# Two attention layers on one core: rounded parts copied ahead of low parts, ScalarE issuing some of the copies, and a longer interleaved tail

## The chip, the cores and the metric

The kernel runs on one core of one Trainium2 chip. The metric is the device time of one execution in microseconds (us); the kernel before has a median of 1974.42 us over three runs (1971.13 to 1975.38). Lower is better.

## The reference, cut to what matters

Two independent attention layers, A and B, each with x of 2048 x 1024, 32 heads of width 32, their own `wqkv` and `wo`. The results stand side by side in the output.

```python
# both: qkv = x @ wqkv, 32 heads of 32; out = attention(q, k, v) @ wo
# A: each query sees 8 keys, 2 apart: pos, pos-2, ..., pos-14  (softmax over those)
# B: each query sees the last 256 keys                         (softmax over those)
return jnp.concatenate([a, b], axis=-1)
```

## The kernel before, in words

**Units.** The work is cut into eight units of 512 positions: four of layer B ("dense", a query sees up to 384 key columns) and four of layer A ("window", 136 key columns; even and odd positions are separated on the host, so 8 keys 2 apart become 8 neighbours). A unit has eight head groups of four heads, so there are 64 head groups, numbered 0 to 63 here in the order of the work. All units but the first of a sequence need the last keys of the unit before, which are kept in a DRAM tile called `halo`.

**Precision by parts.** Every fp32 operand is split into a rounded part and a low part (the remainder). A product is three matmuls (`TERMS`): rounded x rounded, rounded x low, low x rounded. The splitting of inputs is in `Stream.parts` (line 129 the rounding cast on VectorE, lines 134 and 137 the subtraction on GpSimd or VectorE).

**A head group's stages.**

1. Projection (line 363, 24 matmuls of 512 columns for Q and 24 for K). ScalarE writes the rounded part into the tile `nat` (line 314), VectorE the low part (line 318).
2. Stacking (lines 323 to 335). Three DMAs of 256 KB copy `nat` into every third partition of `qst`, three into `kst`. For Q the order is rounded, rounded, low; for K it is rounded, low, rounded. All are issued by SyncE (SP), once both parts of `nat` are counted as done. For K of a unit with a halo, three halo reads (line 308) are issued ahead of them; if the next unit needs it, one halo write (line 333) behind them. If the buffer is still used by the head group two before, the whole stacking is put off (`waiting`).
3. First pass (line 614): sixteen score matmuls (96 rows, up to 384 columns). VectorE finds the row maximum (619), ScalarE the sum of exponentials (624). There are four PSUM banks for scores.
4. Row values: logarithm (637), its parts (642 to 645), a transposing matmul (653), a copy on VectorE (657), and a 16 KB DMA into rows 96 and 97 of `qst` (660, SP).
5. Second pass: scores again, now with the row values (696 dense, 509 window), exponential on ScalarE, masks, and the product with V (741, 548) into PSUM; `finish` writes the parts of the result, `ot` (577, 581).
6. Between these, V projections (line 415) and output projections (line 455; one result copied out through the single buffer `ost`, lines 379 and 382, and stored by a DMA that ScalarE issues, line 470).

**What sets the order.** The order of each engine's instructions is fixed when the program is built. `Clock` is a small cost model: `copy` stands for a DMA that SP issues, `load` for one that ScalarE issues, `fetch` for one of GpSimd. The loop at the end of the kernel takes four lists (row values, second passes, first passes, projections) and puts next on TensorE the item whose modelled ready time comes first. A first pass becomes ready at `done["stack"]`, the modelled landing of K's last copy:

```python
one.append(Item(lambda: latest(rs.when(), done["stack"].get((u, s))),
                lambda b=b, j=j: first(b, j), 0.18 if dense else C1))
```

On the chip TensorE goes through this fixed list. If a copy lands later than modelled, TensorE stands still at that first score matmul although projections are left to do.

**The tail.** The last unit's eight output projections are 24 matmuls each, three per head group. `TAIL` of them have their first seven head groups placed early; the eighth, which needs the last head group's result, follows. The output weights come through `wpool`, three buffers.

Of the kernel before, what the change touches and what calls it, by code (L numbers as in the profile page):

```python
# [14 lines left out]
P = 128  # L15
# [10 lines left out]
O_SLOTS = {2: (0, 1), 3: (2, 3), 4: (4, 5), 5: (6, 7)}  # L26
NX, NST = 10, 1
TAIL, LAND, XAT = 2, 0.45, 1
# [4 lines left out]
class Clock:  # L33
# [53 lines left out]
class Stream:  # L87
# [19 lines left out]
    def split_to(self, n):  # L107
        while self.split < min(n, len(self.items)):
            i = self.split
            self.load_to(i + 1)  # L110
            raw, t0 = self.raw.pop(i)
            if self.items[i][0] == "x":
# [10 lines left out]
            end = self.ready[i] if self.items[i][0] != "x" else max(self.ready[i])  # L123
            self.ck.defer(end, lambda n=i + NRAW + 1: self.load_to(n))
# [22 lines left out]
def kernel(ctx, tc, xs, wqk, wv, wo, outs, units):  # L147
# [23 lines left out]
    for u in range(U):  # L171
        for s in range(NG):
# [3 lines left out]
            if s in V_SLOTS:  # L176
                plan.append(("v", u, V_SLOTS[s]))
# [17 lines left out]
    for p in plan:  # L195
        ly = units[p[1]][0]
        if p[0] == "o":
            item(p, "w", wo[ly, p[2]])
# [99 lines left out]
    def qk_items(u, s):  # L298
# [12 lines left out]
        def evac(t, ps, bank):  # L311
# [5 lines left out]
            def low():  # L317
# [5 lines left out]
                def stack():  # L323
                    if t == 1 and has_halo:
                        read_halo()
                    dst, c = (qst[buf], 0) if t == 0 else (kst[buf], 256)
                    for i, a in enumerate((0, 0, 1) if t == 0 else (0, 1, 0)):
                        nc.sync.dma_start(dst[i:96:3, :, c:c + S].bitcast(F32), hl[:, a, :].bitcast(F32))
# [6 lines left out]
                    done["nat"][hg, t] = e2  # L335

                if hg < 2 or hg - 2 in done["o"]:
                    stack()
                else:
                    waiting.setdefault(hg - 2, []).append(stack)  # L340

            ck.defer(r, low)
# [95 lines left out]
    def o_items(u, n):  # L438
        h = {}

        def ready(k):
            if (u * NG + k) not in done["ot"]:
                return None
            if k == 0:
                st.split_to(where["o", u, n] + 1)
                h["r"] = st.ready[where["o", u, n]]
                return latest(rg.when(), h["r"], done["ot"][u * NG])
            return done["ot"][u * NG + k]

        def run(k):  # L450
            if k == 0:
                h["ps"], h["b"] = rg.take()
                h["w"], _ = st.get(where["o", u, n])
            for i, (a, b) in enumerate(TERMS):
                nc.tensor.matmul(h["ps"], h["w"][:, a, k * P:(k + 1) * P], ot[u, k][:, b, :],  # L455
                                 start=(k == 0 and i == 0), stop=(k == NK - 1 and i == 2))
            if k == 3 and (u < U - 1 or n != TAIL - 1):
                st.split_to(where["o", u, n] + 2)

        def after(k):  # L460
            if k == NK - 1:
# [4 lines left out]
                e = copy_out(o, h["ps"], h["b"], rg)  # L466
# [122 lines left out]
    def attention(u, s):  # L589
# [9 lines left out]
        def first(b, j):  # L599
# [18 lines left out]
            def top():  # L618
                nc.vector.tensor_tensor_reduce(ps[:, :n], ps[:, :n], mask[:, cut:full], scale=-1.0, scalar=BIG,  # L619
                                               op0=ALU.add, op1=ALU.min, accum_out=nm)  # L620
                e = ck.use("dve", (n + 80) / 960, ck.now)
# [29 lines left out]
        def rows(hl):  # L651
# [4 lines left out]
            def copy():  # L656
# [3 lines left out]
                nc.sync.dma_start(q[96:98, :, :].bitcast(F32), rt.bitcast(F32))  # L660
                h["rows"] = ck.copy(0.3, e)
# [212 lines left out]
```

## Time and profile before

| | us |
|---|---|
| median of three runs | 1974.42 |
| the profiled execution | 1973.82 |
| its span, first to last instruction | 1972.1 |
| TensorE busy in it | 1924.7 (12608 matmuls) |
| VectorE, ScalarE, GpSimd busy | 1295.7, 957.5, 708.7 |
| mean granted TensorE clock | 0.987 |

The span is what the profile covers; 1.7 us lie around it. A matmul's time in the profile contains its pipeline, so a busy TensorE is not a full one: what one matmul really takes is the distance from its start to the next one's start. "Idle before" at an instruction is the time for which its engine did nothing, and "<-" names what ended it.

### The profile page before, as it was taken

Reading aid. Unit: us, or ns where it says so; the run is one execution under the profiler, and the core shown is the slowest. Engines: PE = TensorE matmul, PEld = TensorE weight load, DVE = VectorE, ACT = ScalarE, POOL = GpSimd, SP = SyncE. Lnnn points to the kernel's source line nnn. Section 1 sums busy time; section 2 is a strip of 40 time slices with the busy share of each in tenths; the row PEclk is TensorE's granted clock in tenths of the full one; section 3 lists DMA queues with packets and bytes.
Section 4 is the critical chain, followed back from the end, with each engine's and each line's share of the span. In section 5 each row is a group of like instructions: output and inputs, shape, how many; then the busy total and the mean of one; then the engine's idle time right before and its main releaser. Section 6 shows DMA issues by size and latency. Waiting matters only on the chain.

```text
span 1972.1 us, 36479 instructions
## 1 busy us (share of the span) xinstructions
PE 1924.7 (98%) x12608; PEld 1619.8 (82%) x12608; DVE 1295.7 (66%) x3762; ACT 957.5 (49%) x3137; POOL 708.7 (36%) x923
## 2 busy tenths in 40 slices
PE   7999999999999999999999999999999999999998
PEld 6878887888877878788878888978888788888886
DVE  5687776678665786567865657655666557666653
ACT  3565554475654656555563344423534334434441
POOL 4334343444433434443443323233332333233221
PEclk9999999999999999999999999999989999999998
DMA  5555546455546465345645647455553565556442
GB/s 176 150 139 153 160 124 178 132 153 157 152 136 174 121 189 149 117 140 148 177 119 146 173 139 196 128 149 170 149 163 116 174 177 162 141 146 172 136 126 75
DMA packets 136502, 294.92 MB, mean 150 GB/s; under 512 B 14464, under 2 KB 42112, under 8 KB 136320
## 3 DMA queue, kind: packets, MB, share of 16 engines
q1 hardware_dynamic: 85632, 124.82, 26.1%
q0 software_dynamic: 40320, 146.82, 22.9%
q10 hardware_dynamic: 10368, 20.98, 2.9%
q8 instruction: 100, 1.64, 0.4%
q14 instruction: 82, 0.67, 0.1%
HBM read 163.58 MB, written 27.26 MB: 97 GB/s over the span
## 4 chain that ended last, share of the span: by engine, by line
PE 84%; DVE 7%; DMA 6%; ACT 2%; issue 1%; SPq 0%; POOL 0%; DVEq 0%; ACTq 0%; POOLq 0%
PE g L363 31%; PE g L455 16%; PE g L415 16%; PE s L614 7%; PE s L696 5%; PE o L741 4%; PE s L509 3%; DMA qst<-rt 3%; PE o L548 2%; DMA kst<-nat 1%; DMA raw<-xs 1%; DVE x L137 1%; DVE w L129 1%; ACT s L624 1%; DVE w L137 1%
## 5 line engine op out<-in xcount | busy, mean ns | idle before, releaser
L363 PE MATMUL g<-x,w 128*128 128x512 f32 x3072 | 801.9, 401 | 8.6 <-DVE w L129 8.0
L134 POOL TENSOR_TENSOR w<-raw,w 128x512 fp32r<-128x512 f32 x225 | 392.5, 1745 | 897.2 <-PE s L614 285.7
L363 PEld LDWEIGHTS g<-x,w 128*128 128x128 f32 x3072 | 562.0, 191 | 110.9 <-DVE w L129 8.4
L624 ACT ACTIVATE s<-s,nm 128x384 f32<-128x384 f32 (+3 forms) x1024 | 452.3, 443 | 231.0 <-DVE nm L619 227.1
L415 PE MATMUL g<-w,x 128*128 128x256 f32 x3072 | 413.3, 285 | 0.0
L415 PEld LDWEIGHTS g<-w,x 128*128 128x128 f32 x3072 | 392.7, 191 | 1.9 <-issue 0.6
L455 PE MATMUL g<-ot,w 128*128 128x512 f32 x1536 | 384.2, 397 | 3.6 <-DVE w L129 2.9
L455 PEld LDWEIGHTS g<-ot,w 128*128 128x128 f32 x1536 | 283.8, 190 | 58.1 <-DVE w L129 3.6
L619 DVE CUSTOM_DVE_ANT_0 s<-s,mask_d 128x384 f32<-128x384 f32 (+2 forms) x512 | 262.0, 556 | 72.9 <-PE s L614 71.5
L614 PE MATMUL s<-kst,qst 96*128 96x384 f32 (+3 forms) x1024 | 238.7, 303 | 16.2 <-ACT s L624 7.1
L701 ACT ACTIVATE pbuf<-s 128x384 f32<-128x384 f32 (+2 forms) x480 | 197.1, 507 | 85.5 <-PE s L696 81.8
L614 PEld LDWEIGHTS s<-kst,qst 96*128 96x128 f32 x1024 | 181.3, 192 | 60.5 <-ACT s L624 18.1
L624 ACT ACTIVATION_READ_ACCUMULATOR s<-s,nm 128x1 f32 x1024 | 210.2, 205 | 0.0
L619 DVE CUSTOM_DVE_ANT_0 s<-s,mask_w 128x136 f32<-128x136 f32 (+1 forms) x512 | 142.4, 322 | 98.4 <-PE s L614 96.8
L129 DVE CAST w<-raw 128x1024 fp32r<-128x1024 f32 x256 | 199.9, 781 | 9.4 <-PE g L455 9.4
L137 DVE TENSOR_TENSOR w<-raw,w 128x512 fp32r<-128x512 f32 x287 | 197.2, 696 | 8.8
L682 POOL TENSOR_SCALAR_AFFINE_SELECT pbuf<-pbuf 128x128 f32<-128x128 f32 (+1 forms) x383 | 147.9, 404 | 150.1 <-ACT pbuf L701 143.5
L314 ACT ACTIVATE nat<-g 128x512 fp32r<-128x512 f32 x128 | 76.6, 598 | 255.2 <-PE g L363 247.8
L318 DVE SCALAR_TENSOR_TENSOR nat<-g,nat 128x512 fp32r<-128x512 f32 x128 | 88.3, 690 | 145.5 <-ACT nat L314 134.9
L524 DVE TENSOR_TENSOR pbuf<-pbuf,keep_w 128x272 f32<-128x272 f32 (+1 forms) x224 | 116.9, 566 | 61.5 <-ACT pbuf L514 60.6
L619 DVE DVE_READ_ACCUMULATOR2_ANT nm<- 128x1 f32 x1024 | 144.3, 141 | 0.0
L696 PEld LDWEIGHTS s<-qst,kst 98*128 98x128 f32 x704 | 106.2, 189 | 37.8 <-PE o L741 10.0
(48 smaller groups left out, 1227.3 us busy)
## 6 DMA issues: line engine op xcount, KB each, us to landing
raw<-wqk POOLq DMA_DIRECT2D x126, 512.0 KB, 3.7
qst<-nat SPq DMA_DIRECT2D x192, 256.0 KB
kst<-nat SPq DMA_DIRECT2D x192, 256.0 KB
raw<-wo POOLq DMA_DIRECT2D x64, 512.0 KB, 3.7
raw<-wv POOLq DMA_DIRECT2D x62, 512.0 KB, 4.5
outs<-ost ACTq DMA_DIRECT2D x64, 256.0 KB
raw<-xs POOLq DMA_DIRECT2D x28, 512.0 KB, 4.8
halo<-nat SPq DMA_DIRECT2D x40, 256.0 KB
```

The source lines that it names most:

```text
L129: nc.vector.tensor_copy(t[:, 0, :], raw)
L134: nc.gpsimd.tensor_tensor(o, a, b, op=ALU.subtract)
L137: nc.vector.tensor_tensor(o, a, b, op=ALU.subtract)
L363: nc.tensor.matmul(h["ps"], h["w"][:, a, k * P:(k + 1) * P], xt[u][k][:, b, :], start=(k == 0 and i == 0), stop=(k == NK - 1 and i == 2))
L415: nc.tensor.matmul(ps, xt[u][k][:, a, p0:p0 + P], h["w"][:, c, k % kw], start=(k == 0 and i == 0 and r == 0), stop=(k == NK - 1 and i == 2 ...
L455: nc.tensor.matmul(h["ps"], h["w"][:, a, k * P:(k + 1) * P], ot[u, k][:, b, :], start=(k == 0 and i == 0), stop=(k == NK - 1 and i == 2))
L614: nc.tensor.matmul(ps[:, :n], q[0:96, j, b * P:(b + 1) * P], kk[0:96, j, c0:c1], start=True, stop=True)
L619: nc.vector.tensor_tensor_reduce(ps[:, :n], ps[:, :n], mask[:, cut:full], scale=-1.0, scalar=BIG, op0=ALU.add, op1=ALU.min, accum_out=nm)
L624: nc.scalar.activation(ps[:, :n], ps[:, :n], AF.Exp, bias=nm, scale=-1.0, accum_out=sm)
L682: nc.gpsimd.affine_select(w, w, pattern=[[0, m], [step, n]], compare_op=ALU.is_ge, fill=0.0, base=base, channel_multiplier=chan)
L696: nc.tensor.matmul(ps[:, i * n:(i + 1) * n], kk[0:98, j, 256 + kb * P:256 + (kb + 1) * P], q[0:98, j, q0:q0 + n], start=True, stop=True)
L701: nc.scalar.activation(w, ps[:, :pack * n].rearrange("p (j n) -> p j n", j=pack), AF.Exp)
```

## The change

- A new function `place` does the copies of one part. `stack_hi` copies the rounded part, from the moment ScalarE has written it; `stack` copies the low part, from the moment VectorE has. K's two rounded copies now come ahead of its low copy.
- If the buffer is free at that time, the first copy of each Q and K is issued by ScalarE (and modelled by `Clock.load`); the others by SP. In the built program ScalarE issues 32 of Q's and 46 of K's 64 first copies.
- The halo reads are issued ahead of Q's rounded copies rather than ahead of K's.
- The DMA of the row values is issued by ScalarE.
- `done["stack"]` is the later of the modelled landings of the two parts.
- `TAIL` is 4 rather than 2. Output weights 3 to 7 of the last unit go through the x tiles (as two halves), and output 3 through a scores bank.
- In the first unit V's four parts are placed after head groups 0, 2, 4 and 7 rather than 0, 1, 5 and 7; two costs of the model are altered (`fetch`, and VectorE's row maximum).

```diff
-TAIL, LAND, XAT = 2, 0.45, 1
+TAIL, LAND, XAT = 4, 0.45, 1
+V0_SLOTS = {0:0,2:1,4:2,7:3}
...
-        t = max(self.use("pool", 1.0, *ready) + 0.6, self.free["loads"])
+        t = max(self.use("pool", 0.6, *ready) + 0.9, self.free["loads"])
...
-            item(p, "w", wo[ly, p[2]])
+            item(p, "w" if p[1] < U - 1 or p[2] < 3 else "xw", wo[ly, p[2]])
...
                 def stack():
-                    if t == 1 and has_halo:
-                        read_halo()
-                    dst, c = (qst[buf], 0) if t == 0 else (kst[buf], 256)
-                    for i, a in enumerate((0, 0, 1) if t == 0 else (0, 1, 0)):
-                        nc.sync.dma_start(dst[i:96:3, :, c:c + S].bitcast(F32), hl[:, a, :].bitcast(F32))
-                        e2 = ck.copy(0.95, e, ck.now)
+                    e2 = place(1, e)
                     if t == 1:
-                        done["stack"][u, s] = e2
+                        done["stack"][u, s] = max(e2, h2["hi"])
...
+            def place(part, e):
+                dst, c = (qst[buf], 0) if t == 0 else (kst[buf], 256)
+                for i, a in enumerate((0, 0, 1) if t == 0 else (0, 1, 0)):
+                    if a == part:
+                        if i == 0 and h2["now"]:
+                            nc.scalar.dma_start(dst[i:96:3, :, c:c + S].bitcast(F32), hl[:, a, :].bitcast(F32))
+                            e2 = ck.load(0.95, e, ck.now)
+                        else:
+                            nc.sync.dma_start(dst[i:96:3, :, c:c + S].bitcast(F32), hl[:, a, :].bitcast(F32))
+                            e2 = ck.copy(0.95, e, ck.now)
+                return e2
+
+            def stack_hi():
+                if t == 0 and has_halo:
+                    read_halo()
+                h2["hi"] = place(0, r)
...
+            h2 = {"now": hg < 2 or hg - 2 in done["o"]}
+            if h2["now"]:
+                stack_hi()
+            else:
+                waiting.setdefault(hg - 2, []).append(stack_hi)
             ck.defer(r, low)
...
+        ring = rs if last and n == 3 else rg
...
-            if k == 3 and (u < U - 1 or n != TAIL - 1):
-                st.split_to(where["o", u, n] + 2)
+            if k == 3 and (not last or n == 0 or n > 2):
+                st.split_to(where["o", u, n] + (3 if last and n == 0 else 2))
+            if k == 5 and last and n in (1, 2):
+                st.split_to(where["o", u, n] + 3)
...
-                nc.sync.dma_start(q[96:98, :, :].bitcast(F32), rt.bitcast(F32))
-                h["rows"] = ck.copy(0.3, e)
+                nc.scalar.dma_start(q[96:98, :, :].bitcast(F32), rt.bitcast(F32))
+                h["rows"] = ck.load(0.3, e)
```

More of the change, by code (lines that the diff above doesn't have):

```diff
@@ L334, in stack, with later @@
                         e2 = ck.copy(0.95, e, ck.now)
[L335 removed]
+                    done["nat"][hg, t] = max(e2, h2["hi"])
+                later(stack)
+            def place(part, e):
[13 more added lines that the diff above has]
+                h2["hi"] = place(0, r)
+            def later(f):
                 if hg < 2 or hg - 2 in done["o"]:
[L338 removed]
+                    f()
                 else:
[L340 removed]
+                    waiting.setdefault(hg - 2, []).append(f)
+            h2 = {"now": hg < 2 or hg - 2 in done["o"]}
[3 more added lines that the diff above has]
+                waiting.setdefault(hg - 2, []).append(stack_hi)
             ck.defer(r, low)
```

29 lines of the change are left out of this document (17 added, 12 removed).

## The prediction

> **What bounds the kernel now.** I read the page first, then the list of waits by tile, the chain of waits, and timelines of the few places where TensorE stands still.
>
> ```profile
> PE 1924.7 (98%) x12608; PEld 1619.8 (82%) x12608; DVE 1295.7 (66%) x3762; ACT 957.5 (49%) x3137; POOL 708.7 (36%) x923
> PE 84%; DVE 7%; DMA 6%; ACT 2%; issue 1%; SPq 0%; POOL 0%; DVEq 0%; ACTq 0%; POOLq 0%
> ```
>
> TensorE is the bound: 98% busy, 84% of the chain that ended last. Copying faster gains nothing by itself; only TensorE's standing still can go, or grow. Of the time before its score matmuls the view of the tile `kst` gives:
>
> ```profile
>   DMA qst<-rt: 9.1, 14
>   DMA kst<-nat: 5.7, 5
> ```
>
> So before, TensorE waits 5.7 us in all for K's copies and 9.1 us for row values. What such a wait looks like (timeline, K of head group 50):
>
> ```profile
> 1538.17 6.28 PE L455 MATMUL g<-ot,w 128*128 128x512 f32 x27
> 1538.37 0.60 ACT L314 ACTIVATE nat<-g 128x512 fp32r<-128x512 f32 x1 [4.84 <-PE g L363]
> 1539.00 1.93 SPq L328 DMA_DIRECT2D kst<-nat  x3
> 1546.06 0.63 PE L614 MATMUL s<-kst,qst 96*128 96x128 f32 x4 [1.60 <-DMA kst<-nat]
> ```
>
> K's last projection matmul starts at 1537.95. The copies are issued from 1539.00, 1.05 us later; the third has landed at 1545.97, 8.02 us after that matmul. The 27 projections placed between are done 1.60 us too early. The **landing**, from K's last projection matmul to the completion of its last copy, decides, against the **cover**, the matmuls placed between.
>
> The landing, from the completions in the trace, over the 41 head groups whose first copy is issued at once (1.05 to 1.14 us): 6.32 to 9.84 us, median 7.17. The shortest is explained by the DMA engines (view of stretches; TensorE's clock, then DMA share, then GB/s at the end):
>
> ```profile
> 1650.00:1652.40 2.40, 2.40 (x19) 2.28 (x19) 1.80 (x4) 1.96 (x7) 0.65 (x1) 1.00 1.06 217
> ```
>
> While K's three copies of 256 KB run, all 16 engines are busy (share 1.06) at 217 GB/s: 786 KB take 3.6 us. With 1.05 us to the issue, 1.2 to the first packet and 0.5 to the completion this is 6.35, as the shortest ones are. The longer ones have a 512 KB load of weights among them.
>
> **Change, part 1: K's copies.** They stay three, of the same bytes. SP issues a DMA in 0.55 to 0.6 us and its first packet runs 1.20 us after the start of the issue (1.22 in its usual case); a store that ScalarE issues (line 470) takes 0.34 and has its first packet after 0.84. So the data starts 0.36 us earlier. That the low part is issued 0.6 us earlier gives nothing: it queues behind data. New landing, in the middle: 7.17 - 0.36 = 6.81 us, plus 0.15 from landing to the matmul (1545.97 to 1546.06, others up to 0.2): 6.96.
>
> Bounds: no earlier at all (0; not later, since the bytes are the same), or all packets at the fast rate. The first 96 packets of a stacking take 87 ns, the later ones 114 to 219. If two queues kept the fast rate, 24 packets per engine would take 2.1 us rather than 3.3, so the landing would come 0.36 + 1.2 = 1.6 us earlier. I take 0.36, nearest to the row: packets of ScalarE's stores, 85 ns alone, take 127 to 142 ns (medians) where the stack's packets hold most engines. The slowness is shared, not one queue's.
>
> The Trainium skill, "DMA: Bandwidth & Descriptors", section "Issuing engines are not separate DMA queues", speaks against this part: issuing from several engines saves only the issuing time, the same 16 engines do the work. By that rule the gain stays near 0.36 us; by the other bound the sum below would end near 1969.
>
> The cover is read from the order of the two programs, priced by the distance from start to start in the trace: 0.227 us for 512 columns (48 matmuls in 10.88 us), 0.12 for 256 (60 in 7.24), 0.18 and 0.07 for scores of 384 and 136. The altered order puts the first score matmul much earlier. Examples: head group 50 had 28 matmuls of 512 columns (6.7 us), now 25 (6.0); 58 had 37 (8.4), now 25 (5.7); 37 had 54 of 256 and a few small ones (7.1), now 36 (4.9); 0 had 60 of 256 (7.4), now 48 (6.0). Over all: 10 groups had a cover under 7 us, mean 6.7; now 38 have, mean 5.79. The program reckons with a landing 1 to 2 us earlier; the rows give 0.36.
>
> TensorE's wait: 38 x (6.96 - 5.79) = 44.5 us. The same subtraction in before, group by group with its own landing, gives 8.3 (the profile's named waits: 5.7). **+36 us.** With bounds 0 and 1.6 us: +50 and +4 (10 to 12 us of waits remain).
>
> While TensorE waits, the others catch up, so later waits shrink; no row shows by how much. Between 0 and 8 us; I take **-4**. [...] After the 2.0 us of idle before the score matmul at 33.06 (head group 0) the granted clock is 0.89 over 33 to 48, 3.4 us at half speed, 1.7 us lost; after 1.60 us at 1546 it didn't fall. Four more waits over 2 us (groups 26, 27, 37, 42) would cost up to 6.8; **+3**.
>
> **Part 2: row values issued by ScalarE.** In before the issue starts 0.57 us after the transposing matmul where SP is free, and lands 2.3 us later (clean cases, 1.3 of it to the first packet). By ScalarE's 0.84 it lands 0.45 us sooner, if ScalarE is free. The cover now is mostly 3.3 to 7.4 us; five groups have 2.8 or less. Of 9.1 us I let half go: **-4** (bounds -9 and +10). What queues behind it: ScalarE is in order, so exponentials behind the DMA stand until VectorE has copied the row values (0.28 us, plus what VectorE has ahead, up to a 0.78 us cast). 64 times 0.3 to 1 us is 20 to 64 us of ScalarE, at 49% busy; four banks of scores hide it.
>
> ScalarE also gets 78 stack issues: 78 x 0.34 = 27 us, directly behind line 314, waiting for nothing else: nothing on the path. Moving halo reads ahead of Q: SP is past them before K's copies (issued at 1.05 us in most halo groups too); nothing, and at the bound 1.9 us in the few that were blocked, whose cover is over 9 us.
>
> **Part 3: the tail.** In before:
>
> ```profile
> 1917.57 1.60 PE L455 MATMUL g<-ot,w 128*128 128x512 f32 x6
> 1920.52 3.80 PE L509 MATMUL s<-qst,kst 98*128 98x8 f32 x20 [1.36 <-DMA qst<-rt]
> ...
> 1927.09 3.23 PE L455 MATMUL g<-ot,w 128*128 128x512 f32 x6 [0.70 <-ACT ot L577]
> 1933.17 1.22 PE L455 MATMUL g<-ot,w 128*128 128x512 f32 x2 [2.85 <-DVE w L129]
> ```
>
> Start to start beyond the usual pace: 1.5 at 1920, 0.3 at the product with V, 2.0 around 1927 (`ot`), 3.6 at 1933. Now 15 matmuls (3.4 us) instead of 6 cover the row values and 27 (6.1 us) cover `ot`: the first three go, 3.8 us. The last stays: outputs 1 to 3 are copied by VectorE, one after another through the single `ost`. A copy, its store and the landing take about 2.8 us (1929.08 to 1931.83), so the third ends 9.2 us after the first copy starts, and only then does VectorE split output 5's weights (0.45), which TensorE wants after 7.1: 2.6 + 0.4 instead of 3.6. With 0.5 for a shorter time at half clock: **-5** (bounds -9 and 0).
>
> **Part 4: order.** Counting pairs of neighbouring matmuls in both orders, each by its median distance in before, gives 1810.4 and 1806.8 us: **-3.6**. V's new places in the first unit are in this and in part 1. At the unit boundaries, where splits of x bound TensorE, nothing changes.
>
> **Sum**, on the profiled execution's 1973.8: +36 - 4 + 3 - 4 - 5 - 3.6 = 1996.2. The median of three is 0.6 above that execution; I give **1996**.
>
> **Rivals.** (a) *Two queues keep the fast rate*, landing 1.3 to 1.6 us sooner: +8 in part 1, no clock loss, no catching up; 1973.8 + 8 - 4 - 5 - 3.6 = 1969, down to 1962 with parts 2 and 3 at their bounds. This one ends on the other side. It decides from a landing 1.05 us shorter, where the waits (24 us, 15 more than before) equal the gains. For it: the first 96 packets; against it: the shared slowness. Chance 0.22. (b) *ScalarE is held up by the row values*: if the exponentials behind them miss their bank, 64 x 0.3 us = 19 more: 2015. Against it: 49% busy. 0.1. (c) *The change does nothing to the waits on balance*, because the waits only take the place of stands that come later: catching up of 20 us, near 1975. Against it: TensorE is 98% busy, the named waits are few. 0.1. The forecast: 0.58.
>
> **Range and chances.** The forecast's own bounds run from 1980 to 2014 (0 and 0.8 us in part 1); to hold 8 in 10 it must reach into (a): 1963 to 2014. A measurement of this kernel can tell 0.2%, 4 us. Faster by more: (a) and a third of (c), 0.24; within: 0.07; slower: 0.69.
>
> **What would show it.** In the profile after: "PE s <- DMA kst<-nat" and "issue" before the score matmuls rise from 5.7 to over 30 us in some 30 waits; the DMA share while K is copied stays near 1 at 220 GB/s; the waits at `ot` in the tail are gone, one for VectorE's splitting remains near the second last outputs. Landings of 5.5 us or less would make the prediction wrong.

## The result, and the profile after

The changed kernel takes **2048.45 us** (median of four runs, 2041.45 to 2049.67) against 1974.3 for the kernel before on the same chip: ratio 1.0379, interval 1.0353 to 1.0406. The forecast of 1996 had the direction right and the size wrong: +74 us rather than +22. The profiled execution took 2047.95, span 2046.2, mean granted clock 0.983. Line numbers of after: first scores L644, Q/K projection L385, V L437, output L483, `nat` L316 and L320, stacking L341 (ScalarE) and L344 (SP), halo reads L310, row values L690.

The page of after, busy time and the chain that ended last:

```profile
PE 1942.5 (95%) x12608; PEld 1625.6 (79%) x12608; DVE 1274.8 (62%) x3738; ACT 963.0 (47%) x3132; POOL 726.4 (35%) x957
PE 75%; DMA 14%; DVE 5%; ACT 2%; issue 2%; POOL 1%; SPq 0%; ACTq 0%; DVEq 0%; POOLq 0%
```

The number of matmuls is the same, TensorE's share falls from 98% to 95%, and DMA rises from 6% to 14% of the chain. The view of the tile `kst` (idle time, times), two rows of before, then after:

```profile
  ACT s L624: 35.8, 72
  issue: 32.5, 70
```

```profile
  issue: 84.0, 87
  ACT s L654: 57.7, 90
  DMA kst<-nat: 36.0, 24
  DMA qst<-rt: 19.2, 18
  DMA kst<-halo: 10.1, 6
```

K's copies went from 5.7 us in 5 waits to 36.0 in 24, the row values rose from 9.1 to 19.2, "issue" from 32.5 to 84.0, and the waits for ScalarE's work on the score banks from 35.8 to 57.7. The row named after the halo reads, 10.1 us in 6 waits, belongs to K's copies as well. In all six cases the last of the three reads landed only after the matmul had started, so the matmul did not wait for them, and K's own last copy had landed 0.24 to 0.49 us ahead of it. So the first scores stood 46 us in 30 waits for K's copies. These rows overlap, since one stop is booked both for the weight load and for the matmul. So I use another sum below: for each TensorE instruction the distance to the next one's start, less the median distance of the same pair of shapes in before. It adds up to the span. (us; "pace" is the sum of the medians, "half clock" all excess inside stretches of halved clock; smaller rows are left out.)

| | before | after | stacking alone | constants and first unit alone | row values alone | tail alone |
|---|---|---|---|---|---|---|
| first score of a head group | 6.3 | 54.4 | 42.2 | 19.7 | 6.1 | 6.4 |
| first matmul of a second pass | 5.4 | 19.2 | 12.4 | 8.0 | 7.5 | 3.0 |
| transposing matmul of row values | 7.2 | 2.1 | 5.1 | 12.3 | 7.2 | 7.2 |
| other first scores | 20.0 | 24.4 | 23.5 | 11.4 | 24.9 | 21.1 |
| products with V, dense units | 37.6 | 39.2 | 43.5 | 40.1 | 37.6 | 37.6 |
| output projections | 5.7 | 10.6 | 10.2 | 10.7 | 5.7 | 7.6 |
| half clock | 25.5 | 31.4 | 28.6 | 29.5 | 29.2 | 15.4 |
| pace | 1810.4 | 1806.8 | 1807.8 | 1803.5 | 1810.4 | 1810.4 |
| span | 1972.1 | 2046.2 | 2028.7 | 1994.4 | 1982.2 | 1962.5 |

**A group of the plain kind in after** (K of head group 37, timeline; its last projection matmul starts at 1199.38):

```profile
1199.81 0.60 ACT L316 ACTIVATE nat<-g 128x512 fp32r<-128x512 f32 x1 [2.16 <-PE g L385]
1200.43 1.27 SPq L344 DMA_DIRECT2D kst<-nat  x2
1200.44 0.58 ACTq L341 DMA_DIRECT2D kst<-nat  x1
1200.44 0.69 DVE L320 SCALAR_TENSOR_TENSOR nat<-g,nat 128x512 fp32r<-128x512 f32 x1 [0.86 <-ACT nat L316]
...
1205.97 0.63 PE L644 MATMUL s<-kst,qst 96*128 96x128 f32 x4 [1.05 <-DMA kst<-nat]
```

SP and ScalarE issue one copy each at the same moment, 1.05 us after the matmul, SP the low part at 1.78. They land one after another: 4.11, 5.24 and 6.35 us after that matmul. In before such groups took 6.32 to 6.38. Two stretches from the middle of the copies (length, then PE, PEld, DVE, ACT, POOL busy, then clock, DMA share, GB/s):

```profile
1202.80:1204.00 1.20, 1.20 (x12) 1.20 (x12) 0.81 (x6) 1.20 (x7) 0.90 (x2) 1.00 1.08 219
1204.00:1205.20 1.20, 0.92 (x8) 0.72 (x6) 0.00 (x0) 0.57 (x3) 0.46 (x1) 1.00 1.06 210
```

In these, all 16 engines are full at 210 to 219 GB/s, where before showed 217. The start was not won either: in the 20 groups of after that land soonest, the first packet of SP's copy runs 1.20 us after its issue starts, and that of ScalarE's copy, issued at the same moment, 1.87 to 1.89 us. The Trainium skill, "DMA: Bandwidth & Descriptors", section "Issuing engines are not separate DMA queues", said that a second issuing engine saves only issuing time. The trace agrees, and here not even that was saved.

**A group of another kind** (K of head group 39, at a unit's end, timeline of after):

```profile
1248.83 6.75 SPq L344 DMA_DIRECT2D kst<-nat  x2
...
1254.32 0.68 DVE L320 SCALAR_TENSOR_TENSOR nat<-g,nat 128x512 fp32r<-128x512 f32 x1
...
1256.28 3.36 SPq L310 DMA_DIRECT2D kst<-halo  x3
...
1262.41 0.52 PE L644 MATMUL s<-kst,qst 96*128 96x128 f32 x3 [4.09 <-DMA kst<-halo]
```

The rounded copies had landed 6.2 us after the matmul. The low part stood on VectorE behind splits of weights and x until 1254.32, and SP, in order, stood for 5.7 of the 6.75 us until it issued the low copy at 1255.03, with the halo write and reads behind it. The low copy landed at 1262.17, 7.1 us after its issue, beside loads of x and the halo traffic; the reads that the view names are those of the next head group and landed later, the last at 1264.73. TensorE lost 4.09 us with a cover of 10.4.

**The tail of after** (timeline, TensorE, and VectorE's row that ends the wait):

```profile
2010.54 4.95 PE L483 MATMUL s<-ot,x 128*128 128x512 f32 x21
...
2018.04 5.60 PE L483 MATMUL g<-ot,x 128*128 128x512 f32 x24
2025.77 16.88 PE L483 MATMUL g<-ot,x 128*128 128x512 f32 x72 [2.13 <-DVE x L130]
...
2025.30 0.42 DVE L130 CAST x<-raw 128x512 fp32r<-128x512 f32 x1
```

The waits at the row values and at `ot` are gone. One is left, for VectorE's split of output 5's weights behind its third copy through `ost`. Standing in the tail fell from 10.9 us (half clock included) to 2.4.

### The profile page after: what moved, and what is told of

Same layout as the page of the kernel before. It is cut to its first block, busy times and chain, and to the rows that moved or that the text cites. A ratio compares the mean times of both kernels' runs of the same rounds, so it can differ in the third digit from the quotient of the medians.

```text
span 2046.2 us, 36541 instructions
## 1 busy us (share of the span) xinstructions
PE 1942.5 (95%) x12608; PEld 1625.6 (79%) x12608; DVE 1274.8 (62%) x3738; ACT 963.0 (47%) x3132; POOL 726.4 (35%) x957
## 4 chain that ended last, share of the span: by engine, by line
PE 75%; DMA 14%; DVE 5%; ACT 2%; issue 2%; POOL 1%; SPq 0%; ACTq 0%; DVEq 0%; POOLq 0%
PE g L385 29%; PE g L483 14%; PE g L437 12%; PE s L644 7%; DMA kst<-nat 6%; PE s L726 4%; DMA qst<-rt 4%; PE o L771 4%; PE s L539 3%; PE o L578 2%; DMA kst<-halo 1%; DMA raw<-xs 1%; ACT nat L316 1%; DVE nat L320 1%; DVE s L649 1%
## 5 line engine op out<-in xcount | busy, mean ns | idle before, releaser
L385 PE MATMUL g<-x,w 128*128 128x512 f32 x3072 | 795.7, 401 | 9.0 <-DVE w L130 7.9
L135 POOL TENSOR_TENSOR w<-raw,w 128x512 fp32r<-128x512 f32 x228 | 397.2, 1742 | 893.9 <-issue 332.2
L385 PEld LDWEIGHTS g<-x,w 128*128 128x128 f32 x3072 | 564.8, 191 | 117.9 <-DVE w L130 8.2
L437 PE MATMUL g<-w,x 128*128 128x256 f32 x3072 | 420.9, 286 | 0.0
L437 PEld LDWEIGHTS g<-w,x 128*128 128x128 f32 x3072 | 397.3, 192 | 2.3 <-issue 0.8
L483 PE MATMUL g<-ot,w 128*128 128x512 f32 x1416 | 365.0, 401 | 1.4 <-DVE ot L611 1.4
L483 PEld LDWEIGHTS g<-ot,w 128*128 128x128 f32 x1416 | 262.3, 192 | 50.0 <-DVE ot L611 1.8
L644 PE MATMUL s<-kst,qst 96*128 96x384 f32 (+3 forms) x1024 | 240.2, 308 | 62.0 <-DMA kst<-nat 36.0
L644 PEld LDWEIGHTS s<-kst,qst 96*128 96x128 f32 x1024 | 181.4, 195 | 110.8 <-issue 56.5
L712 POOL TENSOR_SCALAR_AFFINE_SELECT pbuf<-pbuf 128x128 f32<-128x128 f32 (+1 forms) x414 | 161.1, 407 | 186.6 <-ACT pbuf L731 182.0
L138 DVE TENSOR_TENSOR w<-raw,w 128x512 fp32r<-128x512 f32 x274 | 192.1, 708 | 8.7
L316 ACT ACTIVATE nat<-g 128x512 fp32r<-128x512 f32 x128 | 76.7, 599 | 250.5 <-PE g L385 203.3
L130 DVE CAST w<-raw 128x1024 fp32r<-128x1024 f32 x251 | 187.1, 745 | 4.7 <-DMA raw<-wv 4.7
L320 DVE SCALAR_TENSOR_TENSOR nat<-g,nat 128x512 fp32r<-128x512 f32 x128 | 88.2, 689 | 152.0 <-ACT nat L316 144.9
L726 PE MATMUL s<-qst,kst 98*128 98x256 f32 (+2 forms) x704 | 134.9, 308 | 12.9 <-DMA qst<-rt 11.1
L554 DVE TENSOR_TENSOR pbuf<-pbuf,keep_w 128x272 f32<-128x272 f32 (+1 forms) x224 | 106.1, 521 | 63.9 <-ACT pbuf L544 62.5
```

What stands on the lines that cost most here:

```text
L130: nc.vector.tensor_copy(t[:, 0, :], raw)
L135: nc.gpsimd.tensor_tensor(o, a, b, op=ALU.subtract)
L138: nc.vector.tensor_tensor(o, a, b, op=ALU.subtract)
L385: nc.tensor.matmul(h["ps"], h["w"][:, a, k * P:(k + 1) * P], xt[u][k][:, b, :], start=(k == 0 and i == 0), stop=(k == NK - 1 and i == 2))
L437: nc.tensor.matmul(ps, xt[u][k][:, a, p0:p0 + P], h["w"][:, c, k % kw], start=(k == 0 and i == 0 and r == 0), stop=(k == NK - 1 and i == 2 ...
L483: nc.tensor.matmul(h["ps"], w[:, a, c:c + P], ot[u, k][:, b, :], start=(k == 0 and i == 0), stop=(k == NK - 1 and i == 2))
```

## The experiments

The kernel before ran beside each call of runs, and its median there was 1966.4 to 1973.8 us; each ratio is taken to the executions of before in the same call, and it can differ by up to 0.2% from the quotient of the medians. The tables of excess compare single traced executions; I read nothing under some 5 us from them.

**1. Order alone, early.** The kernel before, with K's landing modelled earlier:

```diff
-                        done["stack"][u, s] = e2
+                        done["stack"][u, s] = e2 - 1.4
```

> The kernel before with one number altered: the modelled landing of K's last copy is put 1.4 us earlier (done["stack"] = e2 - 1.4). All copies are still issued by SP, in the old order rounded, low, rounded; the row values too. Only the fixed order of the engines changes: 29 head groups now have under 7 us of matmuls between K's last projection and the first score matmul (mean 5.95; before 10, mean 6.7). Theory ORDER (the fixed order counts on a landing that the DMA engines don't give): the landing stays at 6.3 to 9 us, so 29 x (6.95 - 5.95) = 29 us of new standing at the first score matmuls, time 1998 to 2015. Theory SCALARE (what costs is that ScalarE issues copies): nothing that it names is in this kernel, time 1968 to 1982.

2048.5 us, ratio 1.0421 (1.0390 to 1.0452). Its tile `kst`:

```profile
  issue: 99.9, 97
...
  DMA kst<-nat: 36.5, 23
```

With all copies by SP in the old order, a plan that is 1.4 us too hopeful gives as large a loss as the change, with the same 36 us in K's waits. (The edit alters the planned order of all engines, not of TensorE alone.) ScalarE's issuing isn't needed for it. The size was above what I expected: first scores waited 61 us, where the covers gave 29. Of these, 32.5 us lie in 29 groups whose copies are issued late (the first more than 1.2 us, or the third more than 2.6 us, after K's last projection matmul); in before, 25 such groups wait 0.1 us.

**2. Order alone, late.** The changed kernel, with the landing modelled 2.0 us later:

```diff
-                        done["stack"][u, s] = max(e2, h2["hi"])
+                        done["stack"][u, s] = max(e2, h2["hi"]) + 2.0
```

> The changed kernel with one number altered: the modelled landing of K's copies is put 2.0 us later. All issues stay where the change put them, ScalarE's too. Cover under 7 us in 4 head groups, mean 6.8. Theory ORDER: the waits at the first score matmuls fall from 54 us to under 10, time 1995 to 2008 (row values and tail stay as they are). Theory SCALARE: the queue of ScalarE is as full as in the changed kernel, time 2035 to 2055.

1999.7 us, ratio 1.0173 (1.0144 to 1.0203). Its tile `kst`:

```profile
  issue: 32.1, 60
  DMA qst<-rt: 18.7, 13
...
  DMA kst<-nat: 3.5, 2
```

K's waits are gone, more than half of the loss comes back (1.0379 to 1.0173), and the waits for row values stay where the change had them. Some 34 us remain that are not K's copies.

**3 and 4. The changed kernel with ScalarE's issuing undone**, the order of TensorE unchanged: first the stacking copies on `nc.sync`, then only the row values.

```diff
-                            nc.scalar.dma_start(dst[i:96:3, :, c:c + S].bitcast(F32), hl[:, a, :].bitcast(F32))
+                            nc.sync.dma_start(dst[i:96:3, :, c:c + S].bitcast(F32), hl[:, a, :].bitcast(F32))
```

> The changed kernel, TensorE's order the same to the last matmul, but SP issues all copies of Q and K (78 issues go from ScalarE's queue to SP's); the row values stay with ScalarE. Theory ORDER: K's landing is set by the 16 DMA engines and stays at 6.2 to 6.4 us at the shortest, time 2040 to 2056. Theory SCALARE: without 78 issues of 0.58 us in ScalarE's queue the time falls to 2010 or less.

```diff
-                nc.scalar.dma_start(q[96:98, :, :].bitcast(F32), rt.bitcast(F32))
+                nc.sync.dma_start(q[96:98, :, :].bitcast(F32), rt.bitcast(F32))
```

> The changed kernel, TensorE's order the same, but SP issues the row values again (64 issues); the copies stay as changed. In the changed kernel the waits for row values are 19.2 us against 5.4 before, and the issue starts 0.57 to 5.5 us after the transposing matmul, in many groups 0.9 to 2.3 us. Theory ROWS-QUEUE (ScalarE, in order, reaches the issue late): issue at 0.57 us again, 8 to 14 us gained, 2034 to 2040. Rival (the row values wait for DMA engines that are busy with the stack, or the order leaves too little between): no gain beyond 3 us, 2045 to 2051.

Stacking by SP: 2028.6 us, ratio 1.0320 (1.0278 to 1.0362), between what the two theories said; row values by SP: 2046.9, 1.0407 (1.0387 to 1.0428), no gain. (The 5.4 us for before in the second expectation should read 9.1, as in the view of before.) With the stacking on SP the wait for K hardly moves from 36.0 us:

```profile
  DMA kst<-nat: 35.7, 25
```

The excess at the second passes falls from 19 to 8 us and half clock from 31 to 21. ScalarE's list of waits in the changed kernel (total, times, longest) has a row that invites a wrong reading:

```profile
ACT nat L316 <- DMA qst<-nat: 47.0, 10, 5.0
```

The row was 5.0 us before and 19.7 with the stacking on SP. But in all ten cases line 316 starts 0.04 us after the end of the projection's last matmul: ScalarE had waited for the projection, and a copy's signal came in the same moment. So the row does not show ScalarE standing for copies. By the ratios, ScalarE's issuing of the stacking costs about 12 us (1.0379 to 1.0320); by run 2 the early order has more than half of the loss.

**5 and 6. ScalarE's issuing alone**, in the kernel before, TensorE's and VectorE's order untouched: the first copy of each Q and K, and then the row values.

```diff
-                        nc.sync.dma_start(dst[i:96:3, :, c:c + S].bitcast(F32), hl[:, a, :].bitcast(F32))
+                        (nc.scalar if i == 0 else nc.sync).dma_start(dst[i:96:3, :, c:c + S].bitcast(F32), hl[:, a, :].bitcast(F32))
```

> The kernel before with one edit: the first of the three copies of each Q and K is issued by ScalarE; low parts stay where they were, and the order of every TensorE and VectorE instruction is unchanged. Nothing is left out of the computation. ISSUE (my theory now: ScalarE's issuing has a cost of its own, because it takes 0.58 us per copy and ScalarE then stands behind copies that wait): landings of groups that are issued at once keep their shortest value of 6.35 us, ScalarE stands for stacking copies, the time rises by 5 to 15 us. FORECAST (the step of the prediction: the first copy's data starts 0.36 us earlier and nothing waits): landings near 6.0 at the shortest, K's 5.7 us of waits halve, the time falls by 2 to 4 us.

```diff
-                nc.sync.dma_start(q[96:98, :, :].bitcast(F32), rt.bitcast(F32))
+                nc.scalar.dma_start(q[96:98, :, :].bitcast(F32), rt.bitcast(F32))
```

> The kernel before with one edit: the 16 KB copy of the row values is issued by ScalarE; the order of TensorE and VectorE is unchanged. Nothing is left out of the computation. FORECAST (part 2 of the prediction): the wait of 9.1 us for row values falls by half, -4 us. ISSUE: ScalarE reaches the issue later than SP does, because it has exponentials ahead of it, so the issue comes 0.3 us later in the middle and several us later in a few head groups; the waits for row values rise from 9 to about 15 to 20 us, +5 to +10 us.

First copies: 1975.7 us, ratio 1.0041 (1.0025 to 1.0058); the shortest landing is 6.36 us, before 6.32. SP's next issue comes 0.72 us later here, and the first packet of ScalarE's copy runs 1.21 to 1.23 us after its issue in the ten groups that land soonest. Row values: 1982.6, ratio 1.0074 (1.0049 to 1.0100). Both cost, where the prediction had gains.

With the row values on ScalarE the issue still comes 0.57 us after the transposing matmul in the middle, and 1.04 us in the upper quarter (0.88 before). TensorE's waits for row values rose only from 9.1 to 10.4 us, where I expected 15 to 20; other first scores rose by 4.9 and half clock by 3.7, which is at the limit of what one trace tells. How ScalarE itself is held up, at one place in the trace of run 6:

```profile
1225.41 0.27 DVE L657 CAST rt<-s 32x128 fp32r<-32x128 f32 x1
1225.72 0.65 ACTq L660 DMA_DIRECT2D qst<-rt  x1
1226.41 0.34 ACT L624 ACTIVATE s<-s,nm 128x128 f32<-128x128 f32 x1 [4.05 <-DVE nm L619]
```

The row maximum that this exponential needs was done at 1223.18. The exponential stood behind the issue, and the issue behind VectorE's copy of the row values.

Which of TensorE's waits pays for the first copies I could not find: that trace is within 2 us of the trace of before in every row of the table. The traced execution of before took 1973.8 us, 7 more than the median of before beside run 5, so this comparison can't show a cost of 8 us.

**7. The tail alone**, in the kernel before (output 3 may begin only when the last second pass is placed):

```diff
-TAIL, LAND, XAT = 2, 0.45, 1
+TAIL, LAND, XAT = 4, 0.45, 1
...
-            item(p, "w", wo[ly, p[2]])
+            item(p, "w" if p[1] < U - 1 or p[2] < 3 else "xw", wo[ly, p[2]])
...
+            if (u * NG + k) not in done["ot"] or ring is rs and pos["2"] < len(twos):
```

> The kernel before with the change of the tail alone (four interleaved outputs, output weights 3 to 7 of the last unit through the x tiles, output 3 through a scores bank once the last second pass is placed); until the tail the order is unchanged. Nothing is left out. FORECAST (part 3): the waits at the row values and at the last results go, one of 2.3 to 3 us for VectorE's splitting remains near output 4: -5 us, and by the trace of the changed kernel, where 2.4 us of standing is left of 10.9, half clock included, up to -8.5. RIVAL (the waits go elsewhere, for the stores or the weights): within 2 us of before.

1964.0 us, ratio 0.9972 (0.9956 to 0.9987): by the ratio 5.5 us faster, against a forecast of 5; the medians there, 1964.0 and 1966.4, lie only 2.3 us apart. Its timeline has the one wait that was foretold:

```profile
1942.07 16.88 PE L461 MATMUL g<-ot,x 128*128 128x512 f32 x72 [2.13 <-DVE x L129]
```

**8 and 9. Doses on the changed kernel:** the landing 2.0 us later with every copy and the row values back on SP (the edits of 2, 3 and 4 together), and 1.0 us later alone.

> The changed kernel with three edits: the landing of K's copies is modelled 2.0 us later, as in the late-order run, and both the first copies and the row values are issued by SP again; its TensorE order is that of the late-order run, its rounded copies stay ahead of the low ones. Nothing is left out of the computation. ISSUE: of the 31 us by which the late-order run was above before, most goes: 1970 to 1982 on this chip if before gives 1968. RIVAL, QUEUE ORDER (the rounded copies ahead of the low ones are themselves the cost, since SP stands at a low copy that VectorE has not yet written, with halo reads and row values behind it): it stays at 1990 to 2000, with SP's waits for nat and the waits for row values as high as in the late-order run.

> The changed kernel with the landing of K's copies modelled 1.0 us later (2.0 in the late-order run); nothing else, nothing left out. It fills in a row of doses. The covers read from the built order: 21 head groups under 7 us, mean 6.54, against 38 with 5.79 in the changed kernel and 4 with 6.79 at 2.0 us. ORDER: first-score waits fall from 54 to between 12 and 20 us (twice the 8.6 us that the covers give for a landing of 6.95, as in the changed kernel where 44 became 54 and in the early-order run where 29 became 61), time about 2010 to 2020 against the 2048 of the change. RIVAL (it is not the covers): over 2030.

The first: 1990.3 us, ratio 1.0125 (1.0094 to 1.0155). The second: 1997.1, ratio 1.0148 (1.0120 to 1.0175), first-score excess 14.2 as expected from the covers, time lower than either theory said. Between 1.0 and 2.0 us nothing more is gained. The first run agreed with the rival, that rounded copies ahead of low ones cost by themselves; runs 12 and 15 refute it.

**10 to 12. Doses on the kernel before:** the tail with the landing 0.6 us later, the landing 0.7 us earlier, and 2.0 us later; the edit is that of run 1 with `+ 0.6`, `- 0.7`, `+ 2.0`.

> The kernel with the change of the tail alone (1964 us), and K's landing modelled 0.6 us later on top; all copies by SP in the old order, nothing left out. Covers: one group under 7 us, pace of the order 1806.4 against 1810.4. ORDER: the 6 us of first-score waits fall to 2 to 3, the pace gives up to 4: 1956 to 1962. RIVAL (what is given to K's copies is taken from other covers, since the projections are the only cover there is): 1964 to 1972, with more waits for row values.

> The kernel before with K's landing modelled 0.7 us earlier, half the dose of the early-order run (1.4 us, ratio 1.042); nothing else, nothing left out. Covers: 18 groups under 7 us, mean 6.07, 15.9 us short of a landing of 6.95 against 29 at 1.4 us and 2.3 before. ORDER, with what runs have shown (about 80 us for 29 us short, so 2.5 to 3 times the shortage): 35 to 45 us slower, ratio 1.018 to 1.023. RIVAL (the cost is just the shortage, as the prediction reckoned): 12 to 16 us, ratio 1.006 to 1.008.

> The kernel before with K's landing modelled 2.0 us later; copies by SP with the low part of K in the middle, as before; nothing left out. It is the partner of the run with all copies by SP, the rounded ones first and the landing 2.0 us later, which was 1.25% slower than before. No cover under 7 us; pace 1805.7 against 1810.4. LATENESS (scores placed later leave less for the row values and the passes behind them, whatever the order of the copies): 1.0 to 1.5% slower, as that run. QUEUE ORDER (that run was slower because the rounded copies go ahead of the low ones): within 0.4% of before, or faster by up to 8 us (waits of 6 us gone, pace 4.7 less, 3 us more at the row values).

| landing modelled, against before | ratio | interval | first-score excess |
|---|---|---|---|
| 1.4 us earlier | 1.0421 | 1.0390 to 1.0452 | 61.2 |
| 0.7 us earlier | 1.0200 | 1.0179 to 1.0221 | 37.6 |
| as before | 1 | | 6.3 |
| 2.0 us later | 0.9990 | 0.9969 to 1.0011 | 2.7 |
| tail, and 0.6 us later | 0.9942 | 0.9919 to 0.9965 | 10.2 |

Too early costs some 57 us per us; too late costs nothing that can be measured. The dose of 0.7 cost some 40 us, as the rule "2.5 to 3 times the shortage of the covers" said and not the 12 to 16 us of the shortage itself; 18.5 us of it are waits of late groups. The last row is the fastest kernel of the study, 1958.7 us:

```profile
PE 1915.2 (98%) x12608; PEld 1612.1 (82%) x12608; DVE 1272.4 (65%) x3706; ACT 955.7 (49%) x3132; POOL 732.6 (37%) x989
```

A gain over the tail alone isn't shown, since the intervals overlap and the two ran on different chips. In its trace first scores wait more, not less as I expected; pace (1806.4, as expected), half clock (10.9) and other first scores (13.4, against 21.1) are lower.

**13 to 15. The stacking alone**, in the kernel before: whole, with the first copies by ScalarE; then all by SP and modelled so; then that with the landing 2.0 us later.

```diff
-                        if i == 0 and h2["now"]:
-                            nc.scalar.dma_start(dst[i:96:3, :, c:c + S].bitcast(F32), hl[:, a, :].bitcast(F32))
-                            e2 = ck.load(0.95, e, ck.now)
-                        else:
-                            nc.sync.dma_start(dst[i:96:3, :, c:c + S].bitcast(F32), hl[:, a, :].bitcast(F32))
-                            e2 = ck.copy(0.95, e, ck.now)
+                        nc.sync.dma_start(dst[i:96:3, :, c:c + S].bitcast(F32), hl[:, a, :].bitcast(F32))
+                        e2 = ck.copy(0.95, e, ck.now)
```

(The diff leads from run 13 to run 14.)

> The kernel before with the new stacking alone: rounded parts copied first, the first copy of Q and K by ScalarE and modelled so, halo reads ahead of Q. Row values by SP, old tail, old constants; nothing left out. Covers: 38 head groups under 7 us, mean 5.68, 48 us short of a landing of 6.95 (the changed kernel: 38, 5.79, 44). STACKING IS THE CAUSE: first-score waits of 50 to 60 us, ratio 1.035 to 1.045, and what the changed kernel has beside it (row values +7 to +15, tail -6) nearly cancels. RIVAL (first unit, constants and row values carry a part): under 1.025.

> The kernel before with the rounded parts copied ahead of the low ones, all by SP and modelled as SP's copies, halo reads ahead of Q; nothing left out. Covers: 35 groups under 7 us, mean 6.19, 26.5 us short. If the waits follow the shortage as in the doses (16 short gave 42 us, 29 gave 80): 60 to 75 us, ratio 1.03 to 1.038. RIVAL (the copies land earlier in this order, since all three need not wait for the low part): landings 0.5 us shorter, waits near 15 us, ratio under 1.012.

> As the kernel with rounded parts first, all by SP, and K's landing modelled 2.0 us later; no cover under 7 us, pace 1806.6; nothing left out. Its partner with the old order of copies and the same 2.0 us was equal to before (0.999). QUEUE ORDER (SP stands at a low copy that VectorE has not written, with halo reads, the next copies and row values behind it): 1.0 to 1.5% slower than before. RIVAL (the order of the copies costs nothing; the 1.25% of the changed kernel with all copies by SP came from its reckoning, first unit and constants): within 0.3% of before.

Run 13: 2026.8 us, ratio 1.0266 (1.0230 to 1.0302). Run 14: 2002.5, 1.0146 (1.0120 to 1.0172). Run 15: 1976.6, 1.0014 (1.0000 to 1.0028). The tile `kst`, first in run 14, then in run 15:

```profile
  issue: 54.6, 82
...
  DMA kst<-nat: 14.4, 14
```

```profile
  issue: 25.0, 54
...
  DMA kst<-nat: 1.4, 1
```

Rounded before low costs next to nothing once the landing is modelled late enough (run 15, beside 0.9990 in run 12). What costs is that the new reckoning places the scores earlier (35 covers under 7 us, mean 6.19; before 10, 6.72) while the landing gains 0.1 us: the shortest is 6.26 in run 14. Reckoning ScalarE's copies as shorter still (38 covers, mean 5.68), with their issuing, adds another 1.2%. Runs 13 and 14 each ended between their two theories. The rule of 2.5 to 3 times the shortage fails here: 52 and 29 us are 1.1 times the 48 and 26.5 us by which the covers are short. In these two runs the groups that are issued late don't wait (-0.3 and 0.6 us), while they did in runs 1 and 11; why the same hopefulness reaches them only there stays open.

**16 to 18. The first unit and the constants**, in the kernel before: both; V's new places alone; the two constants alone.

```diff
-        t = max(self.use("pool", 1.0, *ready) + 0.6, self.free["loads"])
+        t = max(self.use("pool", 0.6, *ready) + 0.9, self.free["loads"])
...
-                e = ck.use("dve", (n + 80) / 960, ck.now)
+                e = ck.use("dve", (n + 110) / 960, ck.now)
```

(This is the edit of run 18.)

> The kernel before with V's new places in the first unit and the two altered constants of the model alone; nothing left out. Covers: 12 groups under 7 us, mean 6.69, 3.1 us short (before 2.3); pace 1803.5 against 1810.4. PACE (part 4 of the prediction): 4 to 7 us faster, ratio 0.996 to 0.998. RIVAL (what the order gains in pace it loses in covers and row values): within 0.2% of before, or up to 0.5% slower.

> The kernel before with V's new places in the first unit alone; nothing left out. 119 lines of TensorE's order differ from before, 12 covers under 7 us, pace 1807.5 against 1810.4. PLACES: this is the part that costs, 10 to 17 us, ratio 1.005 to 1.009, with late issues of K's copies at the end of the first unit (head group 7). RIVAL (the constants cost, because they alter the order in all units): within 0.2% of before.

> The kernel before with the two constants of the model alone (GpSimd's loads 0.6 + 0.9 us rather than 1.0 + 0.6; VectorE's row maximum 0.03 us longer); nothing left out. 86 lines of TensorE's order differ, 11 covers under 7 us, pace 1805.4 against 1810.4. CONSTANTS: 10 to 17 us slower, ratio 1.005 to 1.009, with the late waits at the starts of units 2 and 4 that the joint run had. RIVAL (the places cost): 2 to 5 us faster by the pace, ratio 0.997 to 1.0.

Both: 1990.9 us, ratio 1.0086 (1.0063 to 1.0109). Places alone: 1973.5, 1.0030 (1.0013 to 1.0048). Constants alone: 1986.6, 1.0085 (1.0057 to 1.0114). I had not expected any of these above 1.005 when the prediction was made, and run 16 is above both of its theories, run 17 between its two. Two constants of the planner, with no instruction altered, cost some 17 us. What it looks like, in the run with the constants alone (head group 31; SP's timeline, TensorE's, and two stretches as above):

```profile
990.04 1.86 SPq L328 DMA_DIRECT2D qst<-nat  x3
991.94 2.49 SPq L308 DMA_DIRECT2D kst<-halo  x3
994.54 1.89 SPq L328 DMA_DIRECT2D kst<-nat  x3
...
1005.79 0.95 PE L614 MATMUL s<-kst,qst 96*128 96x384 f32 x4 [3.27 <-DMA kst<-nat]
```

```profile
1000.00:1002.00 2.00, 2.00 (x11) 1.75 (x10) 1.77 (x9) 2.00 (x8) 0.00 (x0) 1.00 1.09 217
1002.00:1004.00 2.00, 0.52 (x3) 0.09 (x1) 1.97 (x5) 1.60 (x6) 0.81 (x1) 1.00 1.01 298
```

The stacking of this group is put off until its buffer is free: K's first copy goes out 19.5 us after K's last projection matmul, in before 3.0. Then nine copies go out together, GpSimd issues two 512 KB weight loads beside them (993.55 and 995.68), and the engines are full until 1004. K's last copy lands 10.9 us after its first issue; in before, where the loads nearest to the same group's copies were issued 3 and 5 us after them, it took 7.5. The planner now has 23.7 us of projections between (17.8 in before), and it is still too little.

## Why the prediction was wrong, point by point

The change's four parts, each run alone against before, nearly add up to the whole:

| part | forecast, us | alone, us (ratio x median of before there) | from the interval |
|---|---|---|---|
| 1 stacking | +35 | +53 (1.0266) | 45 to 60 |
| 2 row values by ScalarE | -4 | +15 (1.0074) | 10 to 20 |
| 3 tail | -5 | -5.5 (0.9972) | -9 to -3 |
| 4 order (first unit, constants) | -3.6 | +17 (1.0086) | 12 to 22 |
| sum | +22 | +79 | |
| whole change | | +75 (1.0379) | 70 to 80 |

So three terms of the sum failed, each by some 18 to 21 us: the stacking was too small, and the row values and the order had the wrong sign. That the parts add up is in part luck. Run 6 moves only the issue of the row values; the change also has the planner reckon with it (`load`), which no run tries by itself. And taken out of the changed kernel the same part gives nothing back (run 4).

- **Part 1, the landing.** "So the data starts 0.36 us earlier" failed: plain groups land at 6.35 us as before, the very shortest at 6.19 (6.32). ScalarE's issue of this copy takes 0.58 us and not the 0.34 of its stores, and its first packet runs 1.21 us after the issue (run 5), or 1.88 where SP issues at the same moment, and not 0.84. The bound 0 was right, and the shared slowness that I argued from was there. The middle (6.74 against 6.81) came out right by luck: landings over 7.4 us are 10 of the 48 that are issued in good time, and were 17 of 39, and with all copies on SP (run 14) the middle is 6.76 as well.
- **Part 1, the waits.** "38 x (6.96 - 5.79)" was right in kind: the sign that the prediction named, over 30 us in some 30 waits, came with 46 us in 30. In the run with the stacking alone the excess at the first scores rose by 35.9 us; the forecast was 36. In the whole change it rose by 48. By kinds of group in after: 38 plain groups cost 25 us where the covers gave 36; 10 whose landing was over 7.4 us (loads among the copies) cost 19 where they gave 8; 16 whose copies were issued late cost 10 where they gave nothing, 8 of it in groups 39 and 55, whose low part came late from VectorE. I had measured the landing only over groups that are issued at once, and the late ones are where halo reads, the low part and put-off buffers meet.
- **Catching up, -4 us:** the sign failed. With the stacking alone, other rows of the table rose instead: second passes by 7, products with V by 6, output projections by 4.5, other first scores by 3.5, half clock by 3. The pace gave back 2.6. My reading, which no run tests by itself: a late first score makes its row values, second pass and results late as well, and these have covers of their own that the planner had cut to fit.
- **The clock, +3 us:** the term counted stands of over 2 us, and no run shows such a threshold. In before, stretches of half clock also begin within 2.5 us of stands of 0.97 to 1.8 us, and in run 5 the 2.04 us stand before head group 0's scores has none. The excess at half clock rose by 5.9 us in after, and by 3.1 with the stacking alone.
- **Part 2** failed in sign: alone +15 us, within its upper bound of +10 only at the low end. The step "by ScalarE's 0.84 it lands 0.45 us sooner, if ScalarE is free" failed at its condition and in itself. In after the issue comes 0.87 us after the transposing matmul in the middle and up to 5.5 (before 0.57 and 3.6). Where ScalarE was free, the landing came no sooner: at the shortest 2.86 us after that matmul in run 6, and 2.84 in before. "Four banks of scores hide it" was believed without a row; the timeline of run 6 shows an exponential held up.
- **Part 3** was right in its mechanism: VectorE's third copy through `ost` was to end 9.2 us after the first copy started, and did (2016.20 to 2025.38 in after); the cast that ends the wait begins at 2025.30. The wait itself was 2.13 us where 3.0 were forecast.
- **Part 4** counted pairs of neighbours, and this count was right (-3.6 in the trace of after, -6.9 alone). What it left out is that a new order is also a new set of covers: 27 groups whose copies are issued late wait 14 us in run 16, in before 0.1.
- **The rivals.** "Two queues keep the fast rate" is refuted by the landings. "ScalarE is held up" was a real part (some 12 us by run 3, 15 by run 6) and not the whole cause. Missing was a rival in which the altered order itself misses in places that no short cover shows.

Open: why ScalarE's first copies cost 0.4% with an unaltered order, and what makes up the rest of the 1.25% of run 8, which runs 15, 16 and 7 explain to about 0.7%.

## What to carry to other kernels

When a fixed order was cut to measured latencies, an edit that makes the planner more hopeful must be checked against the landing itself: it cost some 57 us per us too early in runs 1 and 11, and nothing measurable 2 us too late. Price a new order on all groups, each with its own landing, the late and put-off ones above all, and give every reordering a risk of 1% even when no instruction changes. Moving a copy's issue to another engine moves a wait into that engine's queue, and in no run here did it gain. And when a list of waits names a copy, look up when that copy landed: here two such rows named the wrong one.

## What the runs showed of the hardware

Issue times on ScalarE differ by the form of the copy (views of lines L341 and L690 in after; ns, minimum, median, maximum):

```profile
L341 ACTq DMA_DIRECT2D kst<-nat x46: 577/582/637, 24.4 to 1972.7; - x46
...
L690 ACTq DMA_DIRECT2D qst<-rt x64: 621/671/1378, 51.1 to 1999.2; - x64
```

The stores of whole tiles from the same engine took 340 ns. SP's issues of the first two forms took the same in before, 576 and 670 ns in the middle, so for these two forms the engine makes no difference. Two 256 KB copies of K issued within 0.01 us of each other by SP and ScalarE completed 1.12 us apart in the middle of 46 groups of after (0.17 to 3.56). Stretches of half clock go with stands, but not by a plain threshold: in after, eight of the nine stands over 2 us have one that begins within 2 us of their end, and in run 7, with most of the tail's stands gone, before's longest stretch (17.1 us, at 1921.3) has no counterpart and all excess in such stretches falls from 25.5 to 15.4 us.
